# Softmax statistics by two-column reductions, squares on one engine, and a planner with a measured transfer queue

## The chip, the cores and the metric

The kernel runs on one core of a Trainium2 chip. The metric is device time in microseconds (us). Three runs of the kernel before took 993.93, 995.59 and 997.24 us; their median, 995.59 us, is the time to compare with. Engines are named as the profile names them: PE (matmul), PEld (its weight loads), DVE (vector), ACT (scalar), POOL (GpSimd), SP (which only issues transfers here).

## What is computed

The reference is a random-feature attention followed by two feed-forward layers. Cut to what matters:

```python
def phi(x):                                    # q and k, both scaled by 64 ** -0.25
    proj = x @ omega.T                         # 64 -> 128 features
    h = proj - (x * x).sum(-1) / 2
    return np.exp(h - h.max(-1)) / np.sqrt(128)
kv = k_p.T @ v;  z = k_p.sum()                 # per batch (4) and head (8), 576 rows
x = (q_p @ kv) / (q_p @ z + 1e-6)              # 2304 tokens x 512
g = x @ w_gate;  x = (g * sigmoid(g) * (x @ w_val)) @ w_out            # 512 -> 1536 -> 512
h = x @ w_in
out = where(h >= 1, h, where(h <= -1, 0, (h + 1) ** 2 / 4)) @ w_out2    # 512 -> 2048 -> 512
```

The feed-forward weights arrive as 64-bit words and are turned into 32-bit floats on the chip.

## The kernel before, in words

**Order of work.** The program text is written as some hundred small generators (K groups, Q groups, weight conversions, feed-forward steps and so on). A planner in the kernel file (class `Planner`, from line 139) plays them through in advance: each yields operations with an engine and an expected cost, and whenever an engine is free in that plan, the waiting operation with the smallest priority number is emitted (`dispatch`, line 225). The emitted order is the order of the instructions on every engine, and an engine never overtakes in its own order. Where an operation may run on either of two engines, `pick` (line 252) compares their load in the plan plus a leaning. So each cost that the planner believes can change the order of everything behind it.

**Transfers in the plan.** All transfers are issued by SP. `dma` (line 366) is three steps: 0.06 us on SP, 0.45 us on a serial stage called HW and bytes/350e3 us on a serial stage called DMA, both served first come, first served, and then 0.9 us until the data may be used.

**Attention.** A group is 256 rows of two heads; there are 72 of them: 36 for K (`k_group`) and 36 for Q (`q_group`). `front` (line 593) projects a group into a PSUM bank (L604, or by three split products, L393 to L395), takes the maximum of each row from there (L624), waits for the sums of squares (`squares`, line 564), makes two small `scalar_tensor_tensor` operations (L626: `st1 = max - sq/16`; L628: `st2 = -sq/16 - st1`, rounded as the reference rounds) and takes the exponential with `st2` as bias, in four ACT instructions (L634) or by a DVE addition and one ACT instruction (L638, L641).

`squares` has three forms, chosen by `pick`: four ACT squares with accumulation (L578), one ACT square of the whole tile and a DVE reduction (L570, L571), or a POOL multiplication and a DVE reduction (L581, L582).

**Feed-forward as filler.** `moe1` (line 1067) runs the first four hidden blocks of the first layer for each of the nine blocks of 256 tokens, as soon as a token block (`x1s`) is ready, at the lowest priority, so that its products fill holes that attention leaves on PE. Step (k, p) needs the weights g and v of hidden blocks 2p and 2p+1, and one step later the two output weights o. The steps come in the order (0,0), (1,0), (1,1), (0,1) and then the rest.

**Early weights.** `conv_feed` (line 468) loads and converts these 12 weights, in the order g0, v0, o0, g1, v1, o1, g2, v2, o2, g3, v3, o3, through two staging buffers (`ws`). The first `N_CS` = 1 may start at once; the rest wait until two of the first Q groups are done (`q0_front`). The first three have priority 0.66, the others 1.10, or 1.20 once the feed-forward has begun. K groups have 0.32 (first batch) or 1.04, Q groups 0.17 or 0.83. A conversion is one ACT operation (L410), four on DVE (L411, L413, L415, L417), and a split into a rounded part (L374 on ACT or L376 on DVE) and a remainder (L384 on POOL or L386 on DVE), after which the weight is ready.

**Later work.** From about 280 us on, attention is done. Then both layers run in blocks of 512 tokens, most of them with a seven-product scheme (`set_up`, line 1346); `row0` and `row1` turn its banks into rows of hidden values, each in a buffer of the ring `hb`.

Of the kernel before, what the change touches and what calls it, by code (L numbers as in the profile page):

```python
# [19 lines left out]
F32 = mybir.dt.float32  # L20
# [53 lines left out]
N_GATE, N_CS = 2, 1  # L74
# [15 lines left out]
W_HI = _bits((1150 << 20) | 0x7FFFF)  # L90

# [20 lines left out]
class Op:  # L112
    def __init__(self, eng, cost, fn, lock=False):
        self.eng, self.cost, self.fn = eng, cost, fn

        self.lock = lock or eng == "POOL"


class Proc:
# [13 lines left out]
    "DMA": {"": 0.9},  # L133
    "HW": {"": 0.65},
    "SP": {"": 0.1},
# [3 lines left out]
class Planner:  # L139


    def __init__(self):
        self.now = 0.0
        self.heap = []
        self.seq = 0
        self.free_at = {}
        self.queue = {}
        self.load = {}
        self.cur = None
        self.port = 0.0  # L150

# [73 lines left out]
    def dispatch(self, eng):  # L225
# [4 lines left out]
        best = q[0] if eng in ("HW", "DMA") else min(q, key=lambda e: (held and e[2].lock, e[1].prio, e[0]))  # L230
# [18 lines left out]
        self.push(end, self.dispatch, eng)  # L249
        self.push(end, self.step, p, None)  # L250

# [29 lines left out]
def performer_moe_kernel(ctx: ExitStack, tc: tile.TileContext, qG, kG, om, ident,  # L281
# [71 lines left out]
    sqr = ring(att, "sqr", 6, [P, 4])  # L353
    xhl = ring(att, "xhl", 2, [P, 2, 256], F32R)
    stat = ring(att, "st", 6, [P, 4, 4])
# [10 lines left out]
    def dma(dst, src, nbytes):  # L366
        yield Op("SP", 0.06, lambda: nc.sync.dma_start(dst, src))
        yield Op("HW", 0.45, None)
        yield Op("DMA", nbytes / 350e3, None)
# [33 lines left out]
    def to_f32(st, src, t):  # L403
# [6 lines left out]
        yield Op("ACT", c_act(512), lambda: nc.scalar.activation(t, hw.bitcast(F32), AF.Abs))  # L410
# [57 lines left out]
    def conv_feed():  # L468
        early = [k for k in w1_keys if k[1] < 2 * NE]
# [17 lines left out]
    def stage(key, t):  # L487
# [3 lines left out]
        yield from dma(w32[key], t, 262144)  # L491
# [72 lines left out]
    def squares(x, sq, x_ev):  # L564
# [3 lines left out]
        how = pl.pick(ACT=0.96, POOL=c_pool(256) + c_dve(256))  # L568
        if SQ3 and how == "POOL" and pl.pick(ACT=c_act(256) + c_dve(256), POOL=c_pool(256) + c_dve(256)) == "ACT":
            yield Op("ACT", c_act(256), lambda: nc.scalar.activation(x, x, AF.Square))  # L570
            yield Op("DVE", c_dve(256), lambda: nc.vector.tensor_reduce(  # L571
                out=sq, in_=x.rearrange("p (u d) -> p u d", u=4), axis=AX.X, op=ALU.add))
            return
        if how == "ACT":
            def acc4():
                for u in range(4):
                    xu = x[:, u * 64:(u + 1) * 64]
                    nc.scalar.activation(xu, xu, AF.Square, accum_out=sq[:, u:u + 1])  # L578
            yield Op("ACT", 0.96, acc4)
        else:  # L580
            yield Op("POOL", c_pool(256), lambda: nc.gpsimd.tensor_tensor(out=x, in0=x, in1=x, op=ALU.mult))  # L581
# [11 lines left out]
    def front(xt, xn, is_q, res, nat, xn_ev, buf):  # L593

        sq = yield Get(sqr)
# [12 lines left out]
        else:  # L608
# [14 lines left out]
        st = yield Get(stat)  # L623
        yield Op("DVE", c_dve(512), lambda: nc.vector.tensor_reduce(out=st[:, 0], in_=psv, axis=AX.X, op=ALU.max))  # L624
        yield sq_end
        yield Op("DVE", 0.08, lambda: nc.vector.scalar_tensor_tensor(  # L626
            out=st[:, 1], in0=sq, scalar=-0.0625, in1=st[:, 0], op0=ALU.mult, op1=ALU.add), True)
        yield Op("DVE", 0.08, lambda: nc.vector.scalar_tensor_tensor(  # L628
            out=st[:, 2], in0=sq, scalar=-0.0625, in1=st[:, 1], op0=ALU.mult, op1=ALU.subtract), True)
        pl.put(sqr, sq)  # L630
        if pl.pick(ACT=4 * 0.25, DVE=c_dve(512)) == "ACT":
            def expo():
                for u in range(4):
                    nc.scalar.activation(e[:, u * P:(u + 1) * P], ps[:, u * P:(u + 1) * P], AF.Exp, bias=st[:, 2, u:u + 1])  # L634
            yield Op("ACT", 4 * 0.25, expo)
            pl.put(bank, ps)
        else:
            yield Op("DVE", c_dve(512), lambda: nc.vector.tensor_tensor(  # L638
                out=e.rearrange("p (u m) -> p u m", u=4), in0=psv, in1=st[:, 2].unsqueeze(2).to_broadcast([P, 4, P]), op=ALU.add))
# [996 lines left out]
```

## Time and profile before

| | |
|---|---|
| median of three runs | 995.59 us |
| lowest, highest | 993.93, 997.24 us |
| span of the profiled execution | 992.6 us |
| PE busy | 969.5 us, 98% |
| DVE, ACT, POOL busy | 833.3, 566.8, 124.9 us |

No separate time is shown for the profiled execution: its span of 992.6 us, from the first to the last instruction, stands for it, 3.0 us below the median. In the rows below, a timeline row gives the start and the duration in us, the engine, the line, the operation and the tiles written and read; neighbours of one kind are merged (x4). A row by line and shape gives the count, then total busy us and the mean ns of one, and behind the last bar the idle time just before them and what ended it. A matmul's recorded end is modelled and overlaps the next one's start.

### The profile page before, as it was taken

The page shows a single profiled execution, that of the slowest core. Times are in us where ns is not written, and L with a number is a line of the kernel's source. Part 1 is how long each engine was busy: PE and PEld are TensorE (multiplying, and loading weights), DVE is VectorE, ACT ScalarE, POOL GpSimd, SP SyncE. Part 2 cuts the span into 40 slices and gives each one's busy share as a digit, 9 for nine tenths or more (in the row PEclk, how much of TensorE's full clock was granted, in tenths as well). Part 3 has the DMA queues.
Part 4 walks back from the last instruction along what each step waited for, and adds up shares of the span by engine and source line. Part 5 has one row for each costly group of instructions (what it writes and reads, how often), then busy time and mean ns, then how long its engine had stood idle before and what let it go on. Part 6 is the DMA issues. An engine that isn't in the chain of part 4 may idle for free.

```text
span 992.6 us, 18444 instructions
## 1 busy us (share of the span) xinstructions
PE 969.5 (98%) x6778; PEld 900.5 (91%) x6778; DVE 833.3 (84%) x1687; ACT 566.8 (57%) x1322; POOL 124.9 (13%) x141
## 2 busy tenths in 40 slices
PE   8889998999999999999999999999999999999998
PEld 7778998999999999999998999999999889999986
DVE  7999898888899999999999999997778668866553
ACT  7997687876755644455535456564546355544331
POOL 2543446533320000000000000000000000000000
PEclk9999999999999999999999999999999999999999
DMA  9765556355467556575556665344313041303022
GB/s 312 231 196 173 171 167 229 124 170 192 149 225 219 194 180 208 169 242 189 191 183 223 217 217 192 96 156 131 110 51 128 1 138 44 128 1 107 1 85 85
DMA packets 90666, 154.49 MB, mean 156 GB/s; under 512 B 8528, under 2 KB 42320, under 8 KB 90576
## 3 DMA queue, kind: packets, MB, share of 16 engines
q1 hardware_dynamic: 90576, 153.32, 47.1%
q8 instruction: 53, 0.87, 0.4%
q14 instruction: 37, 0.30, 0.1%
HBM read 110.30 MB, written 42.99 MB: 154 GB/s over the span
## 4 chain that ended last, share of the span: by engine, by line
PE 80%; DVE 9%; DMA 4%; ACT 3%; issue 2%; SPq 0%; POOL 0%; DVEq 0%; ACTq 0%
PE bank L393 24%; PE bank L395 24%; PE bank L394 24%; PE bank L604 3%; PE bank L680 2%; PE bank L825 1%; DMA xq<-x1d 1%; DMA ws<-in_w_dram 1%; PE bank L818 1%; DMA ki<-in_kG_dram 1%; PE bank L765 1%; DVE wt L415 1%; DVE st L624 1%; DVE wt L417 1%; ACT ebq L634 1%
## 5 line engine op out<-in xcount | busy, mean ns | idle before, releaser
L393 PE MATMUL bank<-x1s,w 128*128 128x256 f32 x442 | 125.4, 284 | 1.5 <-DVE qt L777 1.4
L395 PE MATMUL bank<-x1s,w 128*128 128x256 f32 x442 | 123.5, 280 | 0.0
L394 PE MATMUL bank<-x1s,w 128*128 128x256 f32 x442 | 123.5, 279 | 0.0
L393 PE MATMUL bank<-x1s,wx 128*128 128x256 f32 x328 | 93.1, 284 | 2.4 <-ACT eb L374 1.4
L395 PE MATMUL bank<-x1s,wx 128*128 128x256 f32 x328 | 92.5, 282 | 0.5 <-POOL wx L384 0.5
L394 PE MATMUL bank<-x1s,wx 128*128 128x256 f32 x328 | 92.4, 282 | 0.0
L393 PEld LDWEIGHTS bank<-x1s,w 128*128 128x128 f32 x442 | 83.1, 188 | 5.7 <-DVE qt L777 1.6
L394 PEld LDWEIGHTS bank<-x1s,w 128*128 128x128 f32 x442 | 83.1, 188 | 3.6
L374 ACT ACTIVATE x1s<-xq 128x512 fp32r<-128x512 f32 x85 | 53.2, 628 | 54.9 <-PE bank L395 24.1
L395 PEld LDWEIGHTS bank<-x1s,w 128*128 128x128 f32 x442 | 83.0, 188 | 0.0
L393 PE MATMUL bank<-x1s,wb 128*128 128x256 f32 x286 | 80.0, 280 | 0.0
L395 PE MATMUL bank<-x1s,wb 128*128 128x256 f32 x286 | 79.9, 279 | 0.0
L394 PE MATMUL bank<-x1s,wb 128*128 128x256 f32 x286 | 79.9, 279 | 0.0
L374 ACT ACTIVATE eb<-bank 128x512 f32<-128x512 f32 x93 | 55.0, 591 | 28.7 <-PE bank L395 28.4
L386 DVE TENSOR_TENSOR x1s<-xq,x1s 128x512 fp32r<-128x512 f32 x90 | 61.8, 686 | 10.1 <-ACT x1s L374 10.1
L393 PEld LDWEIGHTS bank<-x1s,wx 128*128 128x128 f32 x328 | 62.1, 189 | 6.7 <-ACT eb L374 1.6
L394 PEld LDWEIGHTS bank<-x1s,wx 128*128 128x128 f32 x328 | 62.2, 190 | 3.7
L395 PEld LDWEIGHTS bank<-x1s,wx 128*128 128x128 f32 x328 | 62.3, 190 | 0.7 <-POOL wx L384 0.7
L393 PEld LDWEIGHTS bank<-x1s,wb 128*128 128x128 f32 x286 | 54.1, 189 | 4.1
L394 PEld LDWEIGHTS bank<-x1s,wb 128*128 128x128 f32 x286 | 53.8, 188 | 4.1
L410 ACT ACTIVATE wt<-ws 128x512 f32<-128x512 f32 x68 | 46.0, 677 | 16.8 <-DMA ws<-in_w_dram 10.3
L1251 DVE TENSOR_TENSOR gb<-bank,eb 128x512 f32<-128x512 f32 x64 | 43.9, 686 | 13.7 <-PE bank L395 13.6
(278 smaller groups left out, 3187.5 us busy)
## 6 DMA issues: line engine op xcount, KB each, us to landing
ws<-in_w_dram SPq DMA_DIRECT2D x40, 512.0 KB, 4.6
ws<-in_wo_dram SPq DMA_DIRECT2D x28, 512.0 KB, 4.4
xq<-x1d SPq DMA_DIRECT2D x36, 256.0 KB, 4.8
xq<-x2d SPq DMA_DIRECT2D x36, 256.0 KB, 4.5
qi<-in_qG_dram SPq DMA_DIRECT2D x34, 256.0 KB, 3.2
ki<-in_kG_dram SPq DMA_DIRECT2D x33, 256.0 KB, 3.7
vi<-in_kG_dram SPq DMA_DIRECT2D x28, 192.0 KB, 3.2
x1d<-os SPq DMA_DIRECT2D x18, 256.0 KB, 3.4
```

The lines of the kernel that those rows point to most:

```text
L374: yield Op("ACT", c_act(n), lambda: nc.scalar.activation(dst, src, AF.Copy, scale=1.0 if scale is None else scale))
L386: yield Op("DVE", c_dve(n), lambda: nc.vector.tensor_tensor(out=dst, in0=a, in1=b, op=op), True)
L393: nc.tensor.matmul(ps, l_hi, r_hi, start=first, stop=False, skip_group_check=shared)
L394: nc.tensor.matmul(ps, l_hi, r_lo, start=False, stop=False, skip_group_check=shared)
L395: nc.tensor.matmul(ps, l_lo, r_hi, start=False, stop=last, skip_group_check=shared)
L410: yield Op("ACT", c_act(512), lambda: nc.scalar.activation(t, hw.bitcast(F32), AF.Abs))
L415: yield Op("DVE", c_dve(512), lambda: nc.vector.scalar_tensor_tensor(out=ti, in0=lw, scalar=29, in1=ti, op0=ALU.logical_shift_right, op1=A ...
L417: yield Op("DVE", c_dve(512), lambda: nc.vector.scalar_tensor_tensor(out=ti, in0=hw, scalar=0xC0000000, in1=ti, op0=ALU.bitwise_and, op1=A ...
L604: nc.tensor.matmul(ps[:, t * 256:(t + 1) * 256], xt[:, t * P:(t + 1) * P], omr, start=True, stop=True)
L624: yield Op("DVE", c_dve(512), lambda: nc.vector.tensor_reduce(out=st[:, 0], in_=psv, axis=AX.X, op=ALU.max))
L680: nc.tensor.matmul(kp[:, 2 * pr + a], e[:, u * P:(u + 1) * P], vb[:, vi + (dv if li == 4 else 0), a * 64:a * 64 + P], start=(li == 0 and a ...
L1251: yield Op("DVE", c_dve(512), lambda: nc.vector.tensor_tensor(out=dst, in0=pq(ps), in1=pq(e), op=ALU.add))
```

## The change

It does six things. The sums of squares move from an own ring (`sqr`, removed) into a column of the statistics tile, whose ring grows from 6 to 10. The maximum is written negated beside it, and the two `scalar_tensor_tensor` operations become two DVE `tensor_reduce` operations, each a negated sum over two neighbouring columns of that tile. The POOL form of the squares is gone; a choice is left between the four ACT squares and one ACT square with a DVE reduction. The planner's transfer is now one step on SP (0.45 us, by priority, at most 8 under way) with a serial transfer of bytes/392e3 us and 1.46 us (load) or 0.98 us (store) behind it. The early weights come in the order g0, g1, v0, v1, o0, o1, g2, g3, v2, v3, o2, o3, with three ahead of `q0_front`. And in the later work, rows take their hidden buffers strictly in row order (`hget`). A few planned costs change a little. The diff, cut to its core (stores are marked as such at every call, and every `Get(hbuf)` of a row becomes `hget`):

```diff
-N_GATE, N_CS = 2, 1
+N_GATE, N_CS = 2, 3
...
+C_SP, DMA_BW, N_DMA = 0.45, 392e3, 8
+L_LD, L_ST = 1.46, 0.98
+R_DMA0, T_DMA0 = 1.6, 5.0
...
-    "DMA": {"": 0.9},
-    "HW": {"": 0.65},
-    "SP": {"": 0.1},
+    "SP": {"": 0.03},
...
+        if eng == "SP" and self.under_way >= N_DMA:
+            return
+        best = min(q, key=lambda e: (held and e[2].lock, e[1].prio, e[0]))
...
+        if op.moves is not None:
+            self.under_way += 1
+            at = max(self.moved, end)
+            self.moved = at + op.moves[0] * (R_DMA0 if at < T_DMA0 else 1.0)
+            end = self.moved + op.moves[1]
+            p.last = {eng: end}
+            self.push(end, self.landed)
         self.push(end, self.step, p, None)
+
+    def landed(self):
+        self.under_way -= 1
+        self.dispatch("SP")
...
-    sqr = ring(att, "sqr", 6, [P, 4])
     xhl = ring(att, "xhl", 2, [P, 2, 256], F32R)
-    stat = ring(att, "st", 6, [P, 4, 4])
+    stat = ring(att, "st", 10, [P, 4, 4])
...
-    def dma(dst, src, nbytes):
-        yield Op("SP", 0.06, lambda: nc.sync.dma_start(dst, src))
-        yield Op("HW", 0.45, None)
-        yield Op("DMA", nbytes / 350e3, None)
+    def dma(dst, src, nbytes, store=False):
+        yield Op("SP", C_SP, lambda: nc.sync.dma_start(dst, src), False, (nbytes / DMA_BW, L_ST if store else L_LD))
...
-        yield Op("ACT", c_act(512), lambda: nc.scalar.activation(t, hw.bitcast(F32), AF.Abs))
+        yield Op("ACT", 0.575, lambda: nc.scalar.activation(t, hw.bitcast(F32), AF.Abs))
...
-        early = [k for k in w1_keys if k[1] < 2 * NE]
+        early = [(s, f) for p in range(NE) for s in ("g", "v", "o") for f in (2 * p, 2 * p + 1)]
...
-        how = pl.pick(ACT=0.96, POOL=c_pool(256) + c_dve(256))
-        if SQ3 and how == "POOL" and pl.pick(ACT=c_act(256) + c_dve(256), POOL=c_pool(256) + c_dve(256)) == "ACT":
-            yield Op("ACT", c_act(256), lambda: nc.scalar.activation(x, x, AF.Square))
-            yield Op("DVE", c_dve(256), lambda: nc.vector.tensor_reduce(
-                out=sq, in_=x.rearrange("p (u d) -> p u d", u=4), axis=AX.X, op=ALU.add))
-            return
+        how = pl.pick(ACT=0.96, DVE=c_act(256) + c_dve(256))
         if how == "ACT":
             def acc4():
                 for u in range(4):
                     xu = x[:, u * 64:(u + 1) * 64]
-                    nc.scalar.activation(xu, xu, AF.Square, accum_out=sq[:, u:u + 1])
+                    nc.scalar.activation(xu, xu, AF.Square, scale=0.25, accum_out=sq[:, u:u + 1])
             yield Op("ACT", 0.96, acc4)
         else:
-            yield Op("POOL", c_pool(256), lambda: nc.gpsimd.tensor_tensor(out=x, in0=x, in1=x, op=ALU.mult))
+            yield Op("ACT", c_act(256), lambda: nc.scalar.activation(x, x, AF.Square, scale=0.25))
...
-        sq = yield Get(sqr)
+        st = yield Get(stat)
+        sq = st[:, :, 1]
...
-        st = yield Get(stat)
-        yield Op("DVE", c_dve(512), lambda: nc.vector.tensor_reduce(out=st[:, 0], in_=psv, axis=AX.X, op=ALU.max))
+        yield Op("DVE", c_dve(512), lambda: nc.vector.tensor_reduce(out=st[:, :, 0], in_=psv, axis=AX.X, op=ALU.max, negate=True))
         yield sq_end
-        yield Op("DVE", 0.08, lambda: nc.vector.scalar_tensor_tensor(
-            out=st[:, 1], in0=sq, scalar=-0.0625, in1=st[:, 0], op0=ALU.mult, op1=ALU.add), True)
-        yield Op("DVE", 0.08, lambda: nc.vector.scalar_tensor_tensor(
-            out=st[:, 2], in0=sq, scalar=-0.0625, in1=st[:, 1], op0=ALU.mult, op1=ALU.subtract), True)
-        pl.put(sqr, sq)
-        if pl.pick(ACT=4 * 0.25, DVE=c_dve(512)) == "ACT":
+        for i in range(2):
+            yield Op("DVE", 0.115, lambda: nc.vector.tensor_reduce(
+                out=st[:, :, 2 + i], in_=st[:, :, i:2 + i], axis=AX.X, op=ALU.add, negate=True))
+        if pl.pick(ACT=4 * 0.262, DVE=c_dve(512)) == "ACT":
             def expo():
                 for u in range(4):
-                    nc.scalar.activation(e[:, u * P:(u + 1) * P], ps[:, u * P:(u + 1) * P], AF.Exp, bias=st[:, 2, u:u + 1])
-            yield Op("ACT", 4 * 0.25, expo)
+                    nc.scalar.activation(e[:, u * P:(u + 1) * P], ps[:, u * P:(u + 1) * P], AF.Exp, bias=st[:, u, 3:4])
+            yield Op("ACT", 4 * 0.262, expo)
             pl.put(bank, ps)
         else:
             yield Op("DVE", c_dve(512), lambda: nc.vector.tensor_tensor(
-                out=e.rearrange("p (u m) -> p u m", u=4), in0=psv, in1=st[:, 2].unsqueeze(2).to_broadcast([P, 4, P]), op=ALU.add))
+                out=e.rearrange("p (u m) -> p u m", u=4), in0=psv, in1=st[:, :, 3].unsqueeze(2).to_broadcast([P, 4, P]), op=ALU.add))
...
-        yield Op("DVE", 0.12, lambda: nc.vector.reciprocal(out=rs, in_=tt.rearrange("p (n c) -> p n c", c=32)[:, :, 0]))
+        yield Op("DVE", 0.135, lambda: nc.vector.reciprocal(out=rs, in_=tt.rearrange("p (n c) -> p n c", c=32)[:, :, 0]))
...
+    def hget(row):
+        if len(row) > 2 and row[4] is not None:
+            yield row[4]
+        h = yield Get(hbuf)
+        if len(row) > 2:
+            pl.set(row[5])
+        return h
+
     def elem1(gps, vps, v_ev, row, nt=512):
-        h = yield Get(hbuf)
+        h = yield from hget(row)
...
-    before = None
+    before = got = None
     for m, a, order, sets in passes:
         for j in order:
             for c in sets:
                 n = 2 if m == 1 and j < 4 else 1 if m == 1 else 4 if j < 4 else 2
                 for r in range(n):
-                    rows[m, a, j, c, r] = Ev(), [], before, Ev()
-                    before = rows[m, a, j, c, r][3]
+                    rows[m, a, j, c, r] = Ev(), [], before, Ev(), got, Ev()
+                    before, got = rows[m, a, j, c, r][3], rows[m, a, j, c, r][5]
```

## Rows read from the trace of the kernel before

**Rows 1.** The page: span and busy time of each engine.
```profile
span 992.6 us, 18444 instructions
PE 969.5 (98%) x6778; PEld 900.5 (91%) x6778; DVE 833.3 (84%) x1687; ACT 566.8 (57%) x1322; POOL 124.9 (13%) x141
```

**Rows 2.** Busy time of each engine by stage; the columns stand in the first line.
```profile
core 0: us, PE busy (x) PEld busy (x) DVE busy (x) ACT busy (x) POOL busy (x), PEclk, DMA share, GB/s
30.00:60.00 30.00, 27.36 (x171) 23.54 (x170) 29.18 (x85) 27.39 (x84) 16.03 (x18) 1.00 0.71 221
60.00:110.00 50.00, 45.05 (x314) 41.02 (x312) 46.22 (x113) 39.76 (x131) 22.68 (x22) 1.00 0.64 204
150.00:190.00 40.00, 35.24 (x277) 33.86 (x277) 34.63 (x80) 31.06 (x118) 23.92 (x30) 0.96 0.51 169
190.00:280.00 90.00, 89.94 (x772) 89.74 (x772) 76.80 (x172) 65.22 (x193) 34.91 (x35) 1.00 0.50 168
280.00:990.00 710.00, 706.20 (x4777) 649.86 (x4775) 585.25 (x1074) 349.69 (x636) 0.00 (x0) 1.00 0.43 142
```

**Rows 3.** Timeline of PE: first matmul of each product of step (0,0).
```profile
55.57 0.37 PE L393 MATMUL bank<-x1s,w 128*128 128x256 f32 x1
...
70.15 0.36 PE L393 MATMUL bank<-x1s,w 128*128 128x256 f32 x1
...
74.18 0.36 PE L393 MATMUL bank<-x1s,w 128*128 128x256 f32 x1
...
82.58 0.36 PE L393 MATMUL bank<-x1s,w 128*128 128x256 f32 x1
```

**Rows 4.** Timeline of POOL: remainders of the early weights, and of a token block.
```profile
41.58 1.27 POOL L384 TENSOR_TENSOR w<-wt,w 128x512 fp32r<-128x512 f32 x1 [1.30 <-ACT w L374]
...
65.44 1.27 POOL L384 TENSOR_TENSOR x1s<-os,x1s 128x512 fp32r<-128x512 f32 x1 [1.07 <-ACT x1s L374]
68.22 1.26 POOL L384 TENSOR_TENSOR w<-wt,w 128x512 fp32r<-128x512 f32 x1 [1.51 <-DVE w L376]
71.20 1.29 POOL L384 TENSOR_TENSOR w<-wt,w 128x512 fp32r<-128x512 f32 x1 [0.75 <-DVE w L376]
```

**Rows 5.** Lines and shapes, 0 to 290 us: the small operations on DVE.
```profile
L628 DVE SCALAR_TENSOR_TENSOR st<-sqr,st 128x4 f32<-128x4 f32 x72 | 17.1, 253 | 0.2
L626 DVE SCALAR_TENSOR_TENSOR st<-sqr,st 128x4 f32<-128x4 f32 x72 | 15.9, 239 | 0.3
L844 DVE RECIPROCAL st<-rect 128x8 f32<-128x8 f32 x36 | 6.9, 193 | 0.4
```

**Rows 6.** Lines L628 and L624, 0 to 290 us: shortest, median and longest ns.
```profile
L628 DVE SCALAR_TENSOR_TENSOR st<-sqr,st x72: 108/154/1251, 8.9 to 258.0; 128x4 f32<-128x4 f32 x72
L624 DVE TENSOR_REDUCE st<-bank x72: 646/681/693, 7.7 to 256.0; 128x4 f32<-128x512 f32 x72
```

**Rows 7.** Busy time in 30 to 110 us: L626, L628 (DVE), then L581 (POOL).
```profile
30.00:110.00 80.00, 4.63 (x25) 1.00 0.67 210
...
30.00:110.00 80.00, 5.73 (x25) 1.00 0.67 210
...
30.00:110.00 80.00, 12.84 (x18) 1.00 0.67 210
```

**Rows 8.** Lines and shapes, 0 to 290 us: squares on POOL and on ACT.
```profile
L581 POOL TENSOR_TENSOR ki<-ki 128x256 f32<-128x256 f32 x22 | 14.9, 682 | 16.8 <-DMA ki<-in_kG_dram 15.3 <-DVE st L628 1.4
L581 POOL TENSOR_TENSOR qi<-qi 128x256 f32<-128x256 f32 x19 | 13.1, 692 | 29.8 <-DMA qi<-in_qG_dram 23.2 <-DVE st L628 4.5 <-DVE wt L413 2.0
L570 ACT ACTIVATE ki<-ki 128x256 f32<-128x256 f32 x4 | 1.7, 423 | 2.4 <-DMA ki<-in_kG_dram 2.3
```

**Rows 9.** The chain of waits, 52 to 112 us: one group's four ACT squares.
```profile
67.02 0.94 ACT qi L578 x8
```

**Rows 10.** The chain of waits, 145 to 192 us: a transfer and what it released.
```profile
147.98 6.26 DMA ws<-in_w_dram
154.26 0.67 ACT wt L410
```

More of the change, by code (lines that the diff above doesn't have):

```diff
@@ L112, with __init__ @@
 class Op:
-    def __init__(self, eng, cost, fn, lock=False):
-        self.eng, self.cost, self.fn = eng, cost, fn
+    def __init__(self, eng, cost, fn, lock=False, moves=None):
+        self.eng, self.cost, self.fn, self.moves = eng, cost, fn, moves
         self.lock = lock or eng == "POOL"
@@ L150, in __init__ @@
         self.port = 0.0
+        self.under_way, self.moved = 0, 0.0
     def push(self, t, fn, *a):
@@ L229, in dispatch @@
         held = self.port > self.now + 0.02
-        best = q[0] if eng in ("HW", "DMA") else min(q, key=lambda e: (held and e[2].lock, e[1].prio, e[0]))
+        if eng == "SP" and self.under_way >= N_DMA:
+            return
+        best = min(q, key=lambda e: (held and e[2].lock, e[1].prio, e[0]))
         if held and best[2].lock:
@@ L490, in stage @@
         yield from to_f32(st, w_src(key), t)
-        yield from dma(w32[key], t, 262144)
+        yield from dma(w32[key], t, 262144, True)
         pl.put(wtmp, t)
@@ L864, in num @@
         yield from x1_split(k, d, x)
-        yield from dma(half_block(x1d, k, d), x.rearrange("p (n t) -> p n t", n=2), P * 512 * 4)
+        yield from dma(half_block(x1d, k, d), x.rearrange("p (n t) -> p n t", n=2), P * 512 * 4, True)
         pl.put(osb, x)
@@ L982, in evac1 @@
         pl.cur.rank = 1.0
-        yield from dma(half_block(x2p, k, d), x.rearrange("p (n t) -> p n t", n=2), P * 512 * 4)
+        yield from dma(half_block(x2p, k, d), x.rearrange("p (n t) -> p n t", n=2), P * 512 * 4, True)
         pl.put(rng, x)
@@ L1008, in evac_late @@
         if a < len(SETS1) - 1:
-            yield from dma(x2q[a][kb][:, n, 0:nt], x, P * nt * 4)
+            yield from dma(x2q[a][kb][:, n, 0:nt], x, P * nt * 4, True)
             pl.set(x2p_ready[a + 1, kb, n])
         else:
-            yield from dma(x2d[n // 2][:, n % 2, kb * 512:kb * 512 + nt], x, P * nt * 4)
+            yield from dma(x2d[n // 2][:, n % 2, kb * 512:kb * 512 + nt], x, P * nt * 4, True)
         pl.put(rng, xb)
@@ L1144, in xu_store @@
     def xu_store(m, j, u, t):
-        yield from dma(xud[m, j, u], t.bitcast(F32), 524288)
+        yield from dma(xud[m, j, u], t.bitcast(F32), 524288, True)
         pl.set(xud_ready[m, j, u])
@@ L1281, in row0 @@
         if key[0] == 1:
-            h = yield Get(hbuf)
+            h = yield from hget(rows[key + (0,)])
             yield from tanh(h, gb[:, 0:512], 512)
@@ L1290, in row0 @@
         for i in range(2):
-            g = yield Get(hbuf)
+            g = yield from hget(rows[key + (i,)])
             evs.append(Ev())
@@ L1309, in row1 @@
         if key[0] == 1:
-            h = yield Get(hbuf)
+            h = yield from hget(rows[key + (1,)])
             yield from tanh(h[:, 256:512], cv[:, 0], 256)
@@ L1323, in row1 @@
         for i in range(2):
-            g = yield Get(hbuf)
+            g = yield from hget(rows[key + (2 + i,)])
             gs.append(g)
@@ L1383, in tail_second @@
     def tail_second(row, ps):
-        g = yield Get(hbuf)
+        g = yield from hget(row)
         yield from relu(g, ps, 512)
@@ L1445, in evac2 @@
             pl.set(acc_free[c])
-            yield from dma(ro, x, 262144)
+            yield from dma(ro, x, 262144, True)
         else:
@@ L1453, in evac2 @@
                 yield Op("DVE", c_dve(n), lambda: nc.vector.tensor_tensor(out=x[:, h], in0=acc[c][:, h], in1=pb[:, h], op=ALU.add))
-                last = pl.spawn(dma(ro[:, h], x[:, h], P * 4 * n))
+                last = pl.spawn(dma(ro[:, h], x[:, h], P * 4 * n, True))
             pl.set(acc_free[c])
```

## The prediction

> **What bounds the kernel now.** I read the page first: PE is busy for 969.5 of 992.6 us [rows 1], so all that can be won without changing the matmuls is about 23 us of holes. The busy time by stage then says where they are [rows 2]. From 280 to 990 us PE is idle for 3.8 us in 710, and from 190 to 280 us for 0.06 in 90: nothing to win there, only to lose. Between 30 and 110 us it is idle for 2.64 + 4.95 = 7.6 us, and between 150 and 190 us for 4.8 us. The rest lies at the start, in 110 to 150 us and at the end. In 30 to 110 us DVE is busy for 29.18 + 46.22 = 75.4 of 80 us and ACT for 27.39 + 39.76 = 67.15 [rows 2]: attention is fed by these two engines and PE waits for them, unless it has feed-forward products to run meanwhile.
>
> The timeline of PE shows how little filler there is. The four products of step (0,0) begin at 55.57, 70.15, 74.18 and 82.58 us [rows 3]: 27 us for work that, at the 89.94 us per 772 matmuls of the full stretch [rows 2], takes 4 x 12 x 0.117 = 5.6 us. By the code they are g0, g1, v0, v1. The timeline of POOL says why the second is late: the third converted weight, o0 in the old order, was done at 41.58 + 1.27 = 42.9 us, and the fourth, g1, only at 68.22 + 1.26 = 69.5 us, v1 at 72.5 us [rows 4]. Conversions after the third have a low priority and starve behind attention on DVE. So an output weight that nobody needs before the next step took the early place of g1.
>
> **The change, part by part.** The sum is made against the profiled span, 992.6 us; the median of the runs stands 3.0 us above it, and I add that at the end.
>
> **Order of early weights.** Second and third place go to g1 and v0, and v1 takes the fourth. Nothing is added: the same 12 loads of one kind through the same two staging buffers, with the same three at high priority. Lifting the gate for three instead of one lets the second load pass at the start, the third still waits for a staging buffer. With places kept, g0, g1 and v0 are ready by 42.9 us and v1 by 69.5. Then g1 and v0 (2.8 us of PE) can follow g0 at 57 us, v1 (1.4 us) at 70, and step (1,0), which uses the same weights and whose token block seems complete at 65.44 + 1.27 = 66.7 us [rows 4], right behind (5.6 us). That is 9.8 us of filler before 80 us, for 4.95 us of idle PE in 60 to 110 us. The lower end of the gain is nothing (holes shorter than the order allows for), the upper end all 7.6 us of 30 to 110 us. I take four fifths of the 4.95, **-4.0 us**, because filler will be twice the hole. What is moved ahead is not missed later: from 190 us on PE is full.
>
> **The two small operations.** 144 of them cost 15.9 + 17.1 = 33.0 us of DVE [rows 5], and 50 fall in 30 to 110 us with 4.63 + 5.73 = 10.4 us [rows 7]. The trace has no reduction over eight numbers. Nearest is the reciprocal over eight, 193 ns [rows 5]: 50 x 0.193 = 9.65, a gain of 0.7 us. At best each takes the shortest record, 108 ns [rows 6]: a gain of 5.0 us. At worst each takes the old mean of the slower one, 253 ns: 12.65, a loss of 2.3 us. I take 0.7 us, as the same size of operand. The operations before have a median of 154 and a longest of 1251 ns [rows 6]: the mean is made by a few that were held, for about as long as a POOL operation of 512 columns lasts [rows 4]. The large reduction from PSUM, in the same stretch, never left 646 to 693 ns [rows 6].
> The Trainium skill, "SBUF — State Buffer", section "Who interferes with whom", says that a vector instruction with two SBUF inputs is shut out while GpSimd reads SBUF, and that on this chip a reduction never is. By that rule no new operation is held, which makes the best case the likelier one. Against the change speaks the Trainium skill, "VectorE: DVE Perf Modes", section "Rules for kernel authors": a reduction on a hot path is the slowest vector operation and should be avoided. By that the price would lie at the upper end and the sum would come out 3.0 us higher.
>
> **Squares off POOL.** 41 squares of the two main buffers (14.9 + 13.1 us) go from POOL [rows 8], 18 of them between 30 and 110 us [rows 7]. Each costs ACT 0.423 us in one piece [rows 8], and then the DVE reduction stays, or 0.94 us in four [rows 9], and the DVE reduction goes. For 18 that is 7.6 to 16.9 us of ACT. ACT is idle for 80 - 67.15 = 12.85 us there, so an even mix (12.3 us) is just covered. If the cover is gone, the excess of the four-piece form, 16.9 - 12.85 = 4.0 us, is on the path. What waits behind is the exponential of the same engine, and PE behind that. In return, squares no longer wait for POOL. I charge 0.7 us, which cancels the gain on DVE. The larger ring of statistics tiles replaces two rings of six; it takes no instruction, and I cost it at nothing.
>
> **Transfers in the plan.** No transfer is added or removed, only their order on SP changes. At 147.98 us a weight load is issued that ACT can use only at 154.26 [rows 10], and PE loses 4.8 us in 150 to 190 us, where the granted clock is 0.96 in the mean [rows 2], that is, part of it at the lower level of 1.2 GHz. The old plan gave such a load 0.06 + 0.45 + 524288/350e3 + 0.9 = 2.91 us, the new one 0.45 + 1.34 + 1.46 = 3.25 us if alone: closer to 6.26, but by a tenth of the error only. What remains is that urgent loads overtake stores and weights for later. I take **-1.0 us**. The ends are -4.8 (this stall gone) and +4.8 (another one like it elsewhere).
>
> **Hidden buffers in row order.** After 280 us the second row of a set now waits for the first to take its buffer, about one product later. PE has the next set's products before it meanwhile, so I charge nothing. If that cover failed, each of the sets would show a hole in a stretch that has 3.8 us of them [rows 2].
>
> Sum: -4.0 - 0.7 + 0.7 - 1.0 = -5.0 us. 992.6 - 5.0 = 987.6 us of span, and with 3.0 us **990.6 us**, 0.5% below the median of 995.6.
>
> **The rivals.**
> *ACT becomes the bound.* Place: 30 to 110 us. Squares join a queue that is 84% full, and the four-piece form wins because the planner's leaning favours ACT. It decides once more than (12.85 - 7.6) / (16.9 - 7.6) = 56% of the squares take four pieces. The price is up to 4.0 us, and PE's filler does not help, since its activations need ACT too: the gain of the weights is lost. 995.6 + 4.0 = 999.6 us, slower. For it: a group's ACT squares already stand on the chain of waits [rows 9]. Against it: the planner sees both loads.
> *Filler moved, not gained.* The products run earlier, but the attention groups behind them come later, and the holes return in 110 to 190 us. The sum is then -1.0 + 1.0: 995.6 us, no change. For it: DVE is full at 94% whatever PE does.
> *Held operations were the bound.* No reduction is held, and DVE gains 5.0 us in the stretch where it is fullest, 4.3 more than I took: 986.3 us. For it: the spread of 108 to 1251 ns [rows 6]. The page on SBUF stands behind this one.
> *The stall of 150 to 190 us goes too.* 4.8 instead of 1.0 us: 986.8 us. Against it: the new plan is still 3 us early for that load.
>
> **How the numbers follow.** Forecast 0.35 (its own range 986 to 995), ACT 0.20, filler moved 0.22, held operations 0.13, the later stall 0.10. A measurement of this kernel can tell about 0.3% from no change, 3 us: faster is below 992.6, slower above 998.6 us. Faster: 0.30 of the forecast, the 0.23 of the two larger gains, 0.02 of moved filler: 0.55. Slower: 0.18 of ACT and 0.04 of moved filler: 0.22. Same: the remaining 0.23. Both larger gains together give 982.5 us, and with the upper end of the weights 981; ACT with a second stall gives more than 1000. The range, 981 to 1001 us, leaves out about 0.1 on each side. Since every order after the first changed decision is new, I do not make it narrower.
>
> **What would show it.** Right: step (0,0) takes less than 17 us from its first to its last product; PE's idle time in 60 to 110 us falls to about 1 us; PE holes after 190 us stay as they are; no record of the new reductions is above 0.4 us; ACT stays under 95% in 30 to 110 us. Wrong: the fourth conversion slips behind 75 us; ACT is full and PE waits for exponentials; holes of a microsecond and more appear behind 190 us, at loads or at the rows of hidden values; or the hole of 60 to 110 us only moves to 110 to 190 us.

## The result and the profile after

The changed kernel takes 1004.18 us in the median (1001.42 to 1007.26), the kernel before in the same comparison 995.63 us. The ratio is 1.0085, 95% interval 1.0059 to 1.0111: slower by 0.85%, where 0.5% faster was forecast, and 3.2 us beyond the range. The head of the profile's page:

```profile
span 1002.2 us, 18533 instructions
PE 973.1 (97%) x6778; PEld 902.5 (90%) x6778; DVE 826.4 (82%) x1679; ACT 583.0 (58%) x1516; POOL 101.2 (10%) x101
```

Beside [rows 1]: DVE has 7 us less to do, POOL 24 us less, ACT 16 us more. Busy time by stage of the changed kernel (columns as in [rows 2]), and below it the one stage of the kernel before that [rows 2] do not show alone:

```profile
30.00:60.00 30.00, 26.31 (x158) 23.02 (x157) 26.77 (x84) 28.01 (x121) 8.77 (x8) 0.94 0.68 215
60.00:110.00 50.00, 46.39 (x329) 43.74 (x329) 44.31 (x115) 45.18 (x167) 17.30 (x14) 0.99 0.63 197
150.00:190.00 40.00, 38.60 (x324) 37.78 (x323) 36.10 (x91) 36.90 (x161) 24.94 (x27) 1.00 0.65 205
280.00:650.00 370.00, 358.82 (x2600) 335.89 (x2600) 337.57 (x638) 194.30 (x364) 0.00 (x0) 1.00 0.60 194
```
```profile
280.00:650.00 370.00, 367.47 (x2686) 347.15 (x2685) 348.03 (x660) 197.03 (x366) 0.00 (x0) 1.00 0.60 197
```

The loss is not made in attention. In 150 to 190 us PE is now idle for 1.4 us instead of 4.8 [rows 2], in 60 to 110 us for 3.6 instead of 5.0, in 30 to 60 us for 3.7 instead of 2.6, and up to 280 us 2037 matmuls have run instead of 2008. It is in 280 to 650 us, where the kernel before left PE idle for 2.5 us and the changed one for 11.2: 8.7 us, and 86 matmuls fewer in the same stretch. Nothing was meant to change there but the order of work.

The 8.7 us are not the whole sum. PE's idle time over the span grew by 6.0 us (29.1 instead of 23.1); the other 3.6 us of the longer span are longer busy time for the same 6778 matmuls. A part of that is TensorE's clock: the granted clock is 0.94 in 30 to 60 us and 0.97 in 110 to 150 us, that is, for part of them at the lower level of 1.2 GHz, and 1.00 in 150 to 190 us; before, it was 1.00, 1.00 and 0.96.

What PE waited for after 280 us, before and after (line waited for: us in total, times, longest):

```profile
PE bank L393 <- ACT eb L374: 1.4, 1, 1.4
```
```profile
PE bank L407 <- ACT eb L388: 9.4, 11, 1.8
```

PE waits for an ACT copy (`eb`, from a PSUM bank into SBUF). Why ACT is late shows in its rows by line and shape, 280 to 650 us; the first is of the kernel before:

```profile
L410 ACT ACTIVATE wt<-ws 128x512 f32<-128x512 f32 x37 | 24.8, 670 | 12.2 <-DMA ws<-in_w_dram 7.9 <-DMA ws<-in_wo_dram 4.2
```
```profile
L424 ACT ACTIVATE wt<-ws 128x512 f32<-128x512 f32 x37 | 24.7, 670 | 39.4 <-DMA ws<-in_w_dram 24.6 <-DMA ws<-in_wo_dram 14.7
```

The same 37 conversions of later weights: ACT stood still in front of them for 39.4 us instead of 12.2, until the load had landed. With every kind of load counted, ACT waited for 65.3 us in this stretch instead of 28.3. ACT keeps its order, so a copy that PE needs can stand behind such a wait. One such hole in the chain of waits, 325 to 336 us, and the same moment on the timelines of ACT and PE (start, duration, and in brackets the idle time before):

```profile
328.21 6.19 DMA wtr<-w32g
...
334.43 0.63 ACT w L388
...
335.06 0.49 ACT eb L388
...
335.60 0.39 PE bank L407
```
```profile
333.68 0.66 ACT L424 ACTIVATE wt<-ws 128x512 f32<-128x512 f32 x1 [2.88 <-DMA ws<-in_wo_dram]
334.43 0.63 ACT L388 ACTIVATE w<-wtr 128x512 fp32r<-128x512 f32 x1
334.96 0.58 ACT L388 ACTIVATE eb<-bank 128x512 f32<-128x512 f32 x1
```
```profile
335.60 0.39 PE L407 MATMUL bank<-x1s,w 128*128 128x256 f32 x1 [1.84 <-ACT eb L388]
```

ACT idles for 2.88 us at a weight load, goes on to a second load, of 256 KB, that took 6.19 us to land, and only then does the copy for which PE waits 1.84 us. The chain runs through the second load, so the conversions of the 512 KB loads are not the only late ones. The median from issue to landing of a 512 KB load of input weights is 4.8 us in this stretch (the last two rows; the first is of the kernel before, 4.5):

```profile
ws<-in_w_dram SPq DMA_DIRECT2D x20, 512.0 KB, 4.5
```
```profile
ws<-in_w_dram SPq DMA_DIRECT2D x20, 512.0 KB, 4.8
ws<-in_wo_dram SPq DMA_DIRECT2D x17, 512.0 KB, 5.2
```

### The profile page after: what moved, and what is told of

The parts are those of the page before. It is cut to its first block, busy times and chain, and to the rows that moved or that the text cites. A ratio compares the mean times of both kernels' runs of the same rounds, so it can differ in the third digit from the quotient of the medians.

```text
span 1002.2 us, 18533 instructions
## 1 busy us (share of the span) xinstructions
PE 973.1 (97%) x6778; PEld 902.5 (90%) x6778; DVE 826.4 (82%) x1679; ACT 583.0 (58%) x1516; POOL 101.2 (10%) x101
## 4 chain that ended last, share of the span: by engine, by line
PE 55%; DVE 22%; DMA 12%; ACT 5%; issue 4%; SPq 1%; POOL 0%; DVEq 0%; ACTq 0%
PE bank L407 16%; PE bank L408 16%; PE bank L409 16%; DMA ws<-in_w_dram 3%; DMA ws<-in_wo_dram 2%; PE bank L614 2%; PE bank L687 2%; DVE wt L431 2%; DVE wt L429 2%; DVE x1s L400 1%; PE bank L832 1%; DVE st L633 1%; DVE wt L425 1%; DMA qi<-in_qG_dram 1%; PE bank L772 1%
## 5 line engine op out<-in xcount | busy, mean ns | idle before, releaser
L407 PE MATMUL bank<-x1s,w 128*128 128x256 f32 x492 | 140.1, 285 | 3.0 <-ACT eb L388 1.8
L409 PE MATMUL bank<-x1s,w 128*128 128x256 f32 x492 | 137.5, 279 | 0.0
L408 PE MATMUL bank<-x1s,w 128*128 128x256 f32 x492 | 137.5, 279 | 0.0
L407 PEld LDWEIGHTS bank<-x1s,w 128*128 128x128 f32 x492 | 92.6, 188 | 8.5 <-ACT eb L388 2.0
L408 PEld LDWEIGHTS bank<-x1s,w 128*128 128x128 f32 x492 | 92.5, 188 | 3.8
L409 PEld LDWEIGHTS bank<-x1s,w 128*128 128x128 f32 x492 | 92.4, 188 | 0.0
L407 PE MATMUL bank<-x1s,wx 128*128 128x256 f32 x278 | 79.1, 285 | 3.4 <-ACT eb L388 3.3
L408 PE MATMUL bank<-x1s,wx 128*128 128x256 f32 x278 | 78.4, 282 | 0.0
L409 PE MATMUL bank<-x1s,wx 128*128 128x256 f32 x278 | 78.3, 282 | 0.0
L407 PEld LDWEIGHTS bank<-x1s,wx 128*128 128x128 f32 x278 | 52.6, 189 | 7.9 <-ACT eb L388 4.2
L388 ACT ACTIVATE hlr<-hb 128x512 fp32r<-128x512 f32 x50 | 31.3, 629 | 48.8 <-PE bank L408 35.2
L633 DVE TENSOR_REDUCE st<-bank 128x4 f32<-128x512 f32 x72 | 48.5, 679 | 10.3 <-PE bank L614 9.0
```

The costliest lines, as they stand in the source:

```text
L388: yield Op("ACT", c_act(n), lambda: nc.scalar.activation(dst, src, AF.Copy, scale=1.0 if scale is None else scale))
L407: nc.tensor.matmul(ps, l_hi, r_hi, start=first, stop=False, skip_group_check=shared)
L408: nc.tensor.matmul(ps, l_hi, r_lo, start=False, stop=False, skip_group_check=shared)
L409: nc.tensor.matmul(ps, l_lo, r_hi, start=False, stop=last, skip_group_check=shared)
```

## The experiments

**The theory.** The new planner believes loads to be there too early. The planner adds to each step a lag behind the engine of the step before. With its own lags (in `LAT`: 0.1 us behind SP, 0.65 behind HW, 0.9 behind DMA), the old model gave a 512 KB load 0.06 + 0.1 + 0.45 + 0.65 + 1.50 + 0.9 = 3.66 us, the new one 0.45 + 1.34 + 1.46 + 0.03 = 3.28. By the theory, ACT operations on loaded data are placed that much earlier, and those that then wait hold up PE. **Rivals:** the row order of the hidden buffers; overtaking on SP; or that any new order costs, because the plan's numbers were fitted to the old one.

All runs, with the median, the ratio to the kernel before and its interval, and from the profile, which is of one execution each, PE's idle time in 280 to 650 us (370 less busy):

| run | us | ratio [95%] | PE idle |
|---|---|---|---|
| changed kernel | 1004.2 | 1.0085 [1.0059, 1.0111] | 11.2 |
| e1, load latency 2.96 | 987.4 | 0.9906 [0.9878, 0.9935] | 0.3 |
| e2, old transfer model | 991.4 | 0.9963 [0.9938, 0.9988] | 4.9 |
| e3, no row order | 999.6 | 1.0043 [1.0015, 1.0071] | 8.8 |
| e4, old weight order | 1003.6 | 1.0068 [1.0046, 1.0090] | 8.1 |
| e7, before + new model | 1015.4 | 1.0210 [1.0190, 1.0230] | 14.1 |
| e6, before + new weight order | 994.8 | 1.0002 [0.9985, 1.0019] | 0.9 |
| e8, before, neutral | 997.4 | 1.0036 [1.0022, 1.0050] | 3.6 |
| e9, before + new statistics | 989.6 | 0.9946 [0.9926, 0.9966] | 1.0 |
| e10, old model, shorter lag | 1003.3 | 1.0089 [1.0059, 1.0120] | 6.0 |
| e11, first come first served on SP | 1012.9 | 1.0183 [1.0149, 1.0217] | 18.5 |
| e12, load latency 1.86 | 995.7 | 1.0005 [0.9987, 1.0024] | 7.0 |
| e13, load latency 4.46 | 990.0 | 0.9952 [0.9935, 0.9970] | 2.3 |
| e14, before + later loads | 994.5 | 1.0000 [0.9983, 1.0017] | 0.0 |
| e15, e1 + old weight order | 990.9 | 0.9968 [0.9947, 0.9989] | 0.1 |
| e16, e1 + old statistics | 997.2 | 1.0018 [1.0001, 1.0036] | 0.0 |
| e17, e1 without row order | 987.3 | 0.9928 [0.9906, 0.9949] | 0.7 |
| e19, before, no POOL squares | 994.4 | 1.0002 [0.9989, 1.0015] | 2.7 |
| e20, e1 + old small operations | 994.7 | 0.9999 [0.9987, 1.0010] | 1.1 |

### One number of the plan

e1 alters one planned number of the changed kernel:

```diff
-L_LD, L_ST = 1.46, 0.98
+L_LD, L_ST = 2.96, 0.98
```

> The changed kernel with one number of the planner altered: a load's planned time behind its bytes is 2.96 us instead of 1.46. Theory (late loads): the new plan believes a 512 KB load to be there 3.3 us after its turn on SP, the profile shows 4.8 and more; ACT then stands in front of late loads in 280 to 650 us (39 us of waiting there, 12 before) and PE waits for the copies behind. With the longer figure ACT's wait falls below 15 us, PE's idle time in 280 to 650 us from 11.2 to under 4 us, and the time to 992 to 997 us. Rival (row order of the hidden buffers): nothing of that depends on the loads, 1002 to 1006 us. Rival (any new order costs): 1000 to 1008 us, with the holes in other places.

Measured 987.4 us, below even the theory's range. The same row of ACT, and the stage:

```profile
L424 ACT ACTIVATE wt<-ws 128x512 f32<-128x512 f32 x37 | 24.8, 671 | 10.2 <-DMA ws<-in_wo_dram 6.2 <-DMA ws<-in_w_dram 3.8
```
```profile
280.00:650.00 370.00, 369.66 (x2696) 349.15 (x2695) 351.11 (x665) 203.52 (x378) 0.00 (x0) 1.00 0.60 196
```

ACT's wait fell from 39.4 to 10.2 us and PE's hole from 11.2 to 0.3. The edit gives no engine other work; what moves with the plan is the order, and with it the planner's choices between engines (1553 ACT instructions instead of 1516, 6778 matmuls in both). So the planned landing is the cause of the loss. That the rest of the change is a gain is seen in e2.

e12 and e13 set the same number to 1.86 and 4.46.

> The changed kernel with a planned load latency of 1.86 us instead of 1.46, which gives a 512 KB load about what the old model gave it, 3.65 us. Theory (loads planned too early): most of the loss goes, ACT's wait in 280 to 650 us about 20 us, 990 to 997 us, between the 1004 us at 1.46 and the 987 us at 2.96. Rival (overtaking on SP): 1000 to 1006 us.

> The changed kernel with a planned load latency of 4.46 us. Theory (loads planned too early): at 2.96 us the plan is about as late as the chip (4.8 us for 512 KB), and nothing is left to win; 985 to 990 us, ACT's wait for weight loads under 8 us in 280 to 650 us. If a plan that is too late costs as much as one too early: 991 us and more.

With 1004.2, 995.7, 987.4 and 990.0 us at 1.46, 1.86, 2.96 and 4.46, the time falls and then flattens or rises a little. ACT's wait at e12 was longer than the expected 20 us, at e13 it was gone:

```profile
L424 ACT ACTIVATE wt<-ws 128x512 f32<-128x512 f32 x37 | 24.7, 671 | 36.6 <-DMA ws<-in_w_dram 17.8 <-DMA ws<-in_wo_dram 11.5 <-DMA wtr<-w32p 7.1
```
```profile
L424 ACT ACTIVATE wt<-ws 128x512 f32<-128x512 f32 x38 | 25.4, 668 | 1.0 <-DMA ws<-in_w_dram 1.0
```

So this wait alone does not give the time: at e12 it is nearly as long as in the changed kernel, and the time is 8.5 us shorter. What falls with the time is PE's own wait for the `eb` copies, 9.4 us in the changed kernel, 5.5 in e12 and 0.3 in e1. That such a copy stood behind a load is shown for one hole only. At 4.46 PE waits for no such copy, and most of its 2.3 idle us are in front of DVE operations.

### The transfer model undone and put in alone

e2 puts the old three steps and their lags into the changed kernel; e7 puts the new model into the kernel before.

```diff
-        yield Op("SP", C_SP, lambda: nc.sync.dma_start(dst, src), False, (nbytes / DMA_BW, L_ST if store else L_LD))
+        yield Op("SP", 0.06, lambda: nc.sync.dma_start(dst, src))
+        yield Op("HW", 0.45, None)
+        yield Op("DMA", nbytes / 350e3, None)
```

> The changed kernel with the planner's transfers as before (three steps, served first come first served), all else as changed. Theory (late loads): with its lags the old model gave a 512 KB load 3.66 us, 0.4 more than the new one, and did not let other loads overtake it; the holes of 280 to 650 us go, 990 to 996 us. Rival (row order): the holes stay, 1002 to 1006 us. Rival (any new order costs): 999 to 1008 us.

> The kernel before with only the planner's transfers changed to the new ones. Theory (late loads): this alone brings the holes of 280 to 650 us: ACT waits over 30 us for weight loads there, 1000 to 1007 us. Rival (row order): without it no holes, 992 to 998 us. Rival (any new order costs): 997 to 1006 us.

Measured 991.4 and 1015.4 us: without the new model the change is a gain, and the new model alone loses 20 us, more than any of the expectations had. In e7:

```profile
L425 ACT ACTIVATE wt<-ws 128x512 f32<-128x512 f32 x40 | 26.8, 670 | 42.6 <-DMA ws<-in_w_dram 28.8 <-DMA ws<-in_wo_dram 13.6
```

The row order is not in e7, so it is not needed for the holes. Against the expectation e2 keeps 4.9 us of them, all of it waiting for `eb` copies, with ACT waiting 22.7 us in front of the conversions. Its plan has the load at 3.66 us, still ahead of the chip's 4.8.

### Too early, or overtaking on SP

The new model is shorter, and it lets urgent transfers overtake. e10 shortens the old one, which serves in order; e11 keeps the new latencies and takes the overtaking and the limit of eight away.

```diff
-    "DMA": {"": 0.9},
+    "DMA": {"": 0.4},
```
```diff
-        if eng == "SP" and self.under_way >= N_DMA:
-            return
-        best = min(q, key=lambda e: (held and e[2].lock, e[1].prio, e[0]))
+        best = q[0] if eng == "SP" else min(q, key=lambda e: (held and e[2].lock, e[1].prio, e[0]))
```

> The changed kernel with the old three-step transfers (as in the run with the old model, 991.4 us) and only the last lag shortened from 0.9 to 0.4 us, so that loads are planned as early as in the changed kernel, still first come first served. Theory (loads planned too early): the holes of 280 to 650 us return, ACT waits over 30 us there for weight loads, 998 to 1006 us. Rival (overtaking on SP is what costs): no change, 989 to 995 us.

> The changed kernel with its short planned latencies, but SP serves first come first served and without the limit of eight. Theory (loads planned too early): the holes stay, 999 to 1008 us. Rival (overtaking on SP is what costs): 989 to 995 us.

Both are slow, 1003.3 and 1012.9 us. Serving by priority and the limit of eight together are worth 9 us to the changed kernel (1012.9 against 1004.2), so they are not what costs. For e10 the time is as the theory had it, the place is not: in 280 to 650 us PE is idle for 6.0 us, 1.1 more than in e2, and ACT waits 24.6 us, not over 30. The rest lies in attention: by stage up to 280 us e10 runs 141 + 480 + 616 + 746 = 1983 matmuls, e2 138 + 500 + 658 + 762 = 2058. The two differ in the lag alone, so half a microsecond less cost matmuls in attention too.

e14 asks whether the kernel before would gain from the same cure.

```diff
-    "DMA": {"": 0.9},
+    "DMA": {"": 2.4},
```

> The kernel before with only the last lag of a planned transfer raised from 0.9 to 2.4 us. Theory (loads planned too early): the kernel before suffers from it too, ACT's wait for loads (12 us in 280 to 650 us) and the hole at 154 us shrink, 985 to 992 us. Rival (the better time at 2.96 us is special to the changed kernel, or only a lucky order): 994 to 1001 us.

It did not: 994.5 us. After 280 us all is well, the stage shows no idle PE at all,

```profile
280.00:650.00 370.00, 370.00 (x2722) 350.51 (x2721) 350.70 (x661) 193.72 (x358) 3.10 (x2) 1.00 0.58 191
```

but attention loses what that wins: 135 + 468 + 624 + 749 = 1976 matmuls up to 280 us, the kernel before 142 + 483 + 611 + 772 = 2008. PE's idle time in that stretch was only 2.5 us in the kernel before, and a later plan is no gain in itself. The time is in the range of the expectation's rival, by which the better time at 2.96 us is special to the changed kernel or a lucky order. So it stays open how much of the 4.0 us between e2 and e1 is luck. The loss itself does not look like luck: with the new statistics, the five orders whose plan has a 512 KB load at 3.28 us or less (changed kernel, e3, e4, e10, e11) took 999.6 to 1012.9 us, the six with 3.66 us or more (e1, e2, e12, e13, e15, e17) 987.3 to 995.7.

### Row order

e3 takes it from the changed kernel, e17 from e1.

```diff
     def hget(row):
-        if len(row) > 2 and row[4] is not None:
-            yield row[4]
-        h = yield Get(hbuf)
-        if len(row) > 2:
-            pl.set(row[5])
-        return h
+        return (yield Get(hbuf))
```

> The changed kernel without the row order of the hidden buffers (each row takes a buffer as it comes, as before). Theory (late loads): unchanged within 3 us, 1001 to 1007 us, ACT's wait for weight loads in 280 to 650 us still above 30 us. Rival (row order): the holes of 280 to 650 us go, 992 to 997 us.

> The changed kernel with a planned load latency of 2.96 us (987.4 us) without the row order of the hidden buffers. Predicted at nothing: 986 to 989 us. If the row order costs by itself (removing it from the changed kernel gained 4 us): 982 to 986 us.

999.6 and 987.3 us. With e1 as the base it is worth nothing, as predicted. In the changed kernel 4.6 us go, a miss of the expectation's 3 us, and ACT's wait is 26.5 us, not over 30; 8.8 of 11.2 us of idle PE stay. Why those 4.6 us go was not tested; with the later loads of e17 nothing goes.

### Weight order

e4 takes it from the changed kernel, e15 from e1, e6 puts it into the kernel before.

```diff
-N_GATE, N_CS = 2, 3
+N_GATE, N_CS = 2, 1
...
-        early = [(s, f) for p in range(NE) for s in ("g", "v", "o") for f in (2 * p, 2 * p + 1)]
+        early = [k for k in w1_keys if k[1] < 2 * NE]
```

> The changed kernel with the early weights in the old order and one ahead of the gate. If the new order gains what was predicted (4 us in 60 to 110 us), this takes 1005 to 1010 us and PE is idle for 2 to 4 us more in 30 to 110 us. If it gains nothing: 1001 to 1007 us with the same idle time in that stretch.

> The changed kernel with a planned load latency of 2.96 us (987.4 us) and the early weights in the old order. If the order of the weights is worth the predicted 4 us once the late loads are out of the way: 990 to 993 us and 2 to 4 us more idle PE in 30 to 110 us. If its gain is always given back: 985 to 989 us.

> The kernel before with only the new order of the early weights and three ahead of the gate. By the prediction's step: 4 us less idle PE in 60 to 110 us, 990 to 993 us. Rival (any new order costs): 996 to 1004 us.

Worth 0.6 us in the changed kernel, 3.5 us on e1 (990.9 against 987.4) and nothing in the kernel before. In e6 (994.8 us, between the two expected ranges) the products do come early, and PE is idle for 3.7 us in 60 to 110 us instead of 5.0, but for 90 - 87.74 = 2.3 us in 190 to 280 us, where it was 0.06 [rows 2]. On e1 the gain is there, and not in the stretch where I put it: PE's idle time in 60 to 110 us is 2.46 us with the new order and 2.45 with the old, and up to 280 us 2045 matmuls have run instead of 2023. That is little more than a new order did by itself (next).

### What any new order costs

e8 edits no instruction, only one planned cost, and so the order and a few choices between engines.

```diff
-        yield Op("DVE", 0.12, lambda: nc.vector.reciprocal(
+        yield Op("DVE", 0.135, lambda: nc.vector.reciprocal(
```

> The kernel before with a change that touches no instruction: the planned cost of a small reciprocal is 0.135 us instead of 0.12, so that only the order of work is played through anew. Rival (any new order costs): 998 to 1004 us, since the numbers of the plan suit one order only. Theory (late loads): the plan of the loads is as before, 993 to 998 us.

997.4 us, 0.36% slower, in an interval clear of no change, and within the range of the theory, not that of the rival. So one re-ordering without content moved this kernel by 2.5 us. It is a single sample, others may move it more, and single differences of that size say nothing of a part. Its profile, of the slowest of its ten executions (1001.5 us), has the loss in attention: in 30 to 60 us 130 matmuls at a mean granted clock of 0.89, where the kernel before ran 171 at 1.00. The 20 us of e7 and the 17 between the changed kernel and e1 are far beyond.

### Statistics

e9 puts the new squares, reductions and ring into the kernel before; e16 takes them from e1.

> The kernel before with only the statistics and squares changed. By the prediction's steps B and C gain and price cancel: 993 to 998 us, ACT over 90% busy in 30 to 110 us. Rival (ACT becomes the bound): 998 to 1003 us, PE's idle time in 30 to 110 us up by 3 us and more. Late loads: no holes after 280 us beyond those of before.

> The changed kernel with a planned load latency of 2.96 us (987.4 us) and the statistics and squares of before. In the kernel before, the new statistics alone gained 5 us. If they are what makes this kernel fast: 991 to 995 us. If it is the later planned loads: 985 to 990 us.

They gain 5.2 us (989.6 against 994.9) and 9.8 us (987.4 against 997.2), two and four times the neutral re-ordering and both beyond the expected ranges: the largest gain in the change. e19 and e20 take only the POOL form out of `squares` and leave the small operations and their rings as before.

```diff
-        how = pl.pick(ACT=0.96, POOL=c_pool(256) + c_dve(256))
+        how = pl.pick(ACT=0.96, DVE=c_act(256) + c_dve(256))
...
-            yield Op("POOL", c_pool(256), lambda: nc.gpsimd.tensor_tensor(out=x, in0=x, in1=x, op=ALU.mult))
+            yield Op("ACT", c_act(256), lambda: nc.scalar.activation(x, x, AF.Square))
```

> The kernel before with only the POOL form of the squares taken out (ACT alone, or ACT and DVE); the two small operations and their rings as before. With new small operations as well it took 989.6 us. If moving the squares off POOL makes that gain: 988 to 991 us. If the reductions make it: 994 us and more, as ACT has more to do and nothing is won on DVE.

> The changed kernel with a planned load latency of 2.96 us, squares without POOL, but the two small operations and their rings as before. It stands between 987.4 us (all new) and 997.2 us (squares and small operations as before). If the squares make the difference: 986 to 990 us. If the reductions make it: 994 to 998 us.

994.4 and 994.7 us. Taking the squares off POOL gives nothing in the kernel before and 2.5 us on e1 (997.2 to 994.7), no more than a neutral re-ordering; the reductions give the rest, 4.8 us (994.4 to 989.6) and 7.3 us (994.7 to 987.4). With them went the larger ring, 10 tiles for 6 and 6, and other planned costs (0.115 us for a reduction, 0.08 for an old operation, which the plan also kept apart from POOL's work). No run separates the three, so what of the gain is the operation itself stays open. The reductions in the changed kernel, by line and shape and by shortest, median and longest:

```profile
L636 DVE TENSOR_REDUCE st<-st 128x4 f32<-128x8 f32 x144 | 18.8, 151 | 1.1
```
```profile
L636 DVE TENSOR_REDUCE st<-st x144: 109/154/165, 7.4 to 255.0; 128x4 f32<-128x8 f32 x144
```

144 operations cost 18.8 us instead of 33.0 [rows 5], and the longest is 165 ns instead of 1251 [rows 6] (1272 on the other of the two old lines, L626). They are not faster in the median; the held ones are gone. By the starts and ends in the traces, 57 of the 144 old operations ran beside a POOL operation, and 25 of these took over 300 ns, no other one did; 72 of the 144 reductions ran beside one, and none took above 165 ns. The Trainium skill's rule in "SBUF — State Buffer", "Who interferes with whom", that a reduction is never shut out by GpSimd, agrees with these 72. The Trainium skill's advice against reductions in "VectorE: DVE Perf Modes", "Rules for kernel authors", does not hold for eight numbers beside a busy POOL: 151 ns in the mean against 239 and 253.

## Why the prediction was wrong

**The step that failed is "Transfers in the plan".** It took -1.0 us for the new model, and the runs show a loss: 12.8 us in the changed kernel (e2 to the changed kernel), 20.6 in the kernel before (e7). The step gave the old plan's load 2.91 us and the new one's 3.25, and concluded that the new plan is closer to the chip. The sum left out two lags of the old model, 0.1 and 0.65 us, that stand in `LAT` (the diff shows them as removed; the description of `dma` ahead of the prediction leaves them out too). The old plan had 3.66 us, the new one has 3.28: further from the chip's 4.8, not closer. And I looked for the effect where a hole was visible, in 150 to 190 us, where things did get better. That this hole came from the load was itself only argued: PE's waits there were for ACT and DVE operations, of 1.6, 1.4, 1.0 and 0.8 us. 280 to 990 us I had called a place with "nothing to win there, only to lose", and priced that loss at nothing. The upper end, "another one like it elsewhere", was 4.8 us; there were eleven waits with 9.4 us in sum.

**Order of early weights: right in mechanism, not shown in size.** The four products of step (0,0) begin, on the timeline of PE (first matmul of each):

```profile
57.78 0.37 PE L407 MATMUL bank<-x1s,w 128*128 128x256 f32 x1
...
59.63 0.37 PE L407 MATMUL bank<-x1s,w 128*128 128x256 f32 x1
...
64.41 0.47 PE L407 MATMUL bank<-x1s,w 128*128 128x256 f32 x1
...
71.11 0.36 PE L407 MATMUL bank<-x1s,w 128*128 128x256 f32 x1
```

13.3 us from first to last instead of 27 [rows 3], within the 17 I had named. PE's idle time in 60 to 110 us did not fall to the 1 us I had named, but to 3.6. The stretch behind filled, and a new hole opened (changed kernel by stage, then its chain of waits):

```profile
60.00:100.00 40.00, 39.68 (x283) 37.49 (x282) 38.52 (x104) 37.64 (x132) 13.29 (x11) 1.00 0.58 179
100.00:110.00 10.00, 6.71 (x49) 6.26 (x49) 5.79 (x12) 7.54 (x37) 4.01 (x4) 0.95 0.86 268
110.00:120.00 10.00, 10.00 (x67) 9.18 (x66) 8.49 (x24) 8.67 (x37) 1.49 (x2) 0.88 0.45 142
```
```profile
102.44 5.73 DMA ki<-in_kG_dram
```

PE is idle for 0.3 us in 60 to 100 us (3.8 before), and for 3.3 in the next ten, at a K load of 5.73 us. The hole has a price behind it as well: the granted clock fell to the lower level, 0.95 and 0.88 in the mean of these two rows, by which an estimated 0.5 + 1.2 = 1.7 us of work were lost. Alone the step was worth 0 to 3.5 us, as the base allowed, not 4.

**The two small operations: gain mis-sized.** I took 193 ns, from a reciprocal over eight numbers; they measured 151, between the bounds of 108 and 253. And I counted only the 50 in 30 to 110 us, a gain of 0.7 us, where 144 gave DVE 14.2 us and the kernel 5 to 7. The rival of the held operations fits that part, with the ring and the planned costs as open terms.

**Squares: price too high.** ACT is busy for 28.01 + 45.18 = 73.2 of 80 us in 30 to 110 us, 91%, under the 95% I had named, and e19 shows no loss. The rival "ACT becomes the bound" gave the right direction and nearly the right time, 999.6 us, by a cause that did not happen; that is luck. Moved filler was no cause either, though e6 shows it in small.

**Hidden buffers in row order: right** on e1, 987.3 against 987.4.

The forecast without the transfer model, -4.0 us, compares with e2's 991.4, about -3.6: near, but by luck, as a sum of a smaller and a larger part than I had taken.

## What to carry to other kernels

Where instruction order comes from a plan, an expected landing that is too early can cost more than one too late, as here in the changed kernel (1004.2 us at 1.46, 990.0 at 4.46): the engine that waits for the load also holds everything behind it. Compare planned and measured landing for each size before touching the model, all lags included, and ask of every stage, the saturated ones above all, which engine stands in front of loads. Change such a model alone, and measure a re-ordering without content beside it, to know what size of difference means anything. The version that beats both here is the changed kernel with a planned load latency of 2.96 us: 987.4 us, a ratio of 0.9906 [0.9878, 0.9935] to the kernel before.

## What was not expected of the hardware

A DVE reduction of eight numbers into four took 109 to 165 ns in 144 cases beside a busy POOL, while the two-input operation that it replaces took up to 1272. And a landing planned only 0.4 us earlier, for a 512 KB load that takes 4.8 on the chip, went with 8.5 us of time (e12 to the changed kernel), with the same transfers in both.
